# Local q and k loaded heads side by side and turned by transposes, half of the strided v on GpSimd's queue, one warming product per unit

## The chip, the cores and the metric

The kernel runs on one core of a Trainium2 chip. The metric is the device time of one execution in microseconds (us). Three runs of the kernel before took 1207.23 to 1209.63 us, with a median of 1208.55.

## The reference

An attention layer with two kinds of masked heads feeds two mixture-of-experts layers. Only the attention is touched by the change:

```python
scores = scale * np.matmul(q, k.transpose(0, 1, 3, 2))     # 4 x 8 heads x 576 x 576, head size 64
mask_local = (rel >= 0) & (rel < 32)
mask_strided = (rel >= 0) & (pos[None, :] % 32 == pos[:, None] % 32)
masks = np.stack([mask_local if h < H // 2 else mask_strided for h in range(H)], axis=0)
...
attn = attn / (np.sum(attn, axis=-1, keepdims=True) + 1e-09)
return np.matmul(attn, v)
```

Heads 0 to 3 are local (each query sees the 32 keys up to itself), heads 4 to 7 strided (each sees the keys at its own place modulo 32). The first mixture gives each token to one of 8 experts, with 288 places each, in the order of the logits; the second weighs 4 experts by given shares. All is in float32.

## The kernel before

The function `front` computes the attention of 4 batches in 40 units, 10 for each batch: 5 strided ones (two groups of 108 or 126 rows each), then 5 local ones. A loop over t runs them as a software pipeline. In step t PE does, in this order: warming products, the transposes of the probabilities of unit t-4 (`tr_p`, line 222), the products with v of unit t-5 (`av`, lines 235 and 242), rows and logits of finished units, one piece of q or k (`pre`), the scores of unit t (lines 186 and 189), and one more piece. GpSimd (POOL) scales the probabilities of unit t-2 (`norm`, line 215), ScalarE (ACT) takes the exponentials of unit t-1 (`exps`, line 205), VectorE (DVE) adds the mask and finds the maximum (line 196). [...]

A piece (`piece`) turns a part of q or k so that the head size stands in the partitions. There are 16 for a batch: 8 strided ones, four transposes each (line 153), and 8 local ones, six products with the identity each (line 164). A copy on DVE or ACT (`copy`, lines 134 to 140) then takes the result out of PSUM into its place. The pieces of batch 0's strided heads stand ahead of the loop, those of its local heads in steps 1 to 4. The other batches' pieces begin with the seventh step of the batch before: four steps with strided pieces, four with local ones.

The loads are issued by `load_qk` (q and k: `qs`, `ks` strided, `ql`, `kl` local), `load_v` (strided v, `vs`) and `load_vl` (local v, `vl`), all on SP's queue. Batch 0 and the q, k of batch 1 come first; from then on step 10b+2 issues q, k of batch b+2 and strided v of batch b+1, step 10b+6 the local v of batch b+1. The program gives each load of a queue one of eight semaphores in turn, and a load waits for the one eight before it on its queue.

Warming products (`keep_busy`, line 409) multiply a constant tile `hot` and are read by nobody; they go to the PSUM tile `xr`, of which there are two buffers, shared with rows, logits and tokens. Before, they stand in steps 0 to 7 and, after the 40 units, in steps 41 to 44.

After the front a search on DVE picks the tokens of the experts (lines 522 to 746), the rows go to DRAM, and `experts` does the rest in an order that a planner made when the program was built.

Of the kernel before, what the change touches and what calls it, by code (L numbers as in the profile page):

```python
# [18 lines left out]
FT = mybir.dt.float32  # L19
# [15 lines left out]
def dap(t, off, *dims):  # L35
    return bass.AP(tensor=t.tensor, offset=t.offset + off, ap=[list(d) for d in dims])

def front(tc, ident, hot, q, k, v, wg, dp, xd, L, ready, hold, deferred):
    nc = tc.nc
    B, H, S, D = q.shape  # L40
    hs = S * D
    with ExitStack() as st:
        cst = st.enter_context(tc.tile_pool(name="fc", bufs=1))
        ld = st.enter_context(tc.tile_pool(name="fl", bufs=2))
# [6 lines left out]
        def load_qk(b, kinds="sl"):  # L51
            T = LD.setdefault(b, {})
            if "s" in kinds:
                for nm in ("qs", "ks"):
                    T[nm] = ld.tile([72, 32, 64], FT, name=nm)
            n = 8 if b == 0 else 32
            for r in range(0, 32 if "s" in kinds else 0, n):
                for nm, src in (("qs", q), ("ks", k)):
                    nc.sync.dma_start(T[nm][:, r:r + n].rearrange("p r d -> p (r d)"), dap(src, (b * H + 4) * hs + r * D, [hs, 4], [32 * D, 18], [1, n * D]))
            for nm, src in (("ql", q), ("kl", k)) if "l" in kinds else ():  # L60
                T[nm] = ld.tile([96, 4, 6, 64], FT, name=nm)
                nc.sync.dma_start(T[nm].rearrange("p h r d -> p h (r d)"), dap(src, b * H * hs, [6 * D, 96], [hs, 4], [1, 6 * D]))

        def load_v(b, lo=0, hi=10):
            T = LD[b]
            if not lo:
                T["vs"] = ld.tile([126, 10, 128], FT, name="vs")
            for t, (b0, n) in list(enumerate(zip(starts, sizes)))[lo:hi]:
                p = 0
                while p < n:  # L70
                    h, rp = divmod(b0 + p, 16)
                    m = min(n - p, 16 - rp)
                    nc.sync.dma_start(T["vs"][18 * p:18 * (p + m), t], dap(v, (b * H + 4 + h) * hs + 2 * rp * D, [2 * D, m], [32 * D, 18], [1, 2 * D]))
                    p += m

        def load_vl(b):
            T = LD[b]
            T["vl"] = ld.tile([96, 9, 256], FT, name="vl")
            nc.gpsimd.memset(T["vl"][:32, 0], 0.0)
            nc.sync.dma_start(T["vl"][32:, 0].rearrange("p (h d) -> p h d", d=D), dap(v, b * H * hs, [D, 64], [hs, 4], [1, D]))  # L80
            for h in range(4):
                nc.sync.dma_start(T["vl"][:, 1:, 64 * h:64 * h + 64], dap(v, (b * H + h) * hs + 32 * D, [D, 96], [64 * D, 8], [1, D]))

        load_qk(0)
        load_v(0, 0, 6)
        load_qk(1, "s")
# [33 lines left out]
        units = []  # L120
# [7 lines left out]
        def copy(out, in_, scale=None, eng="p"):  # L128

            flip[0] += 1  # L130
            ch = side_of[eng]
            if ch == "a" or (ch == "f" and flip[0] % 2):
                if scale is None:
                    nc.scalar.copy(out, in_)
                else:
                    nc.scalar.activation(out, in_, AF.Copy, scale=scale)
            elif scale is None:
                nc.vector.tensor_copy(out, in_)
            else:
                nc.vector.tensor_scalar(out, in_, scale, None, op0=OP.mult)  # L140

        def piece(b, i):

            j, i = divmod(i, 8)
            p = ps.tile([128, 512], FT, name="tr", bufs=2)
            sc = 0.125 if j == 0 else None
            if i < 4:
                if i == 0:
                    (QS, KS)[j][b] = wk.tile([128, 4, 16, 18], FT, name=("qS", "kS")[j])
                src, dst = LD[b][("qs", "ks")[j]], (QS, KS)[j][b]  # L150
                for a in range(4):
                    r = 8 * i + 2 * a
                    nc.tensor.transpose(p[:, 72 * a:72 * a + 72], src[:, r:r + 2, :].rearrange("p r d -> p (r d)"), ident[:72, :72])  # L153
                copy(dst[:, :, 4 * i:4 * i + 4, :].rearrange("p h r j -> p r h j"), p[:, :288].rearrange("p (r h j) -> p r h j", r=4, h=4), sc, "q" if sc else "p")
            else:
                hp, a = divmod(i - 4, 2)
                if i == 4:
                    (QL, KL)[j][b] = wk.tile([128, 2, 576 + 32 * j], FT, name=("qL", "kL")[j])
                    if j:
                        nc.gpsimd.memset(KL[b][:, :, :32], 0.0)  # L160
                src, dst = LD[b][("ql", "kl")[j]], (QL, KL)[j][b]
                for t in range(3):
                    for x in range(2):
                        nc.tensor.matmul(p[64 * x:64 * x + 64, 96 * t:96 * t + 96], src[:, 2 * hp + x, 3 * a + t, :], ident[:96, :96], start=True, stop=True)  # L164
                copy(dst[:, hp, 32 * j:].rearrange("p (s a t) -> p a t s", a=2, t=3)[:, a], p[:, :288].rearrange("p (t s) -> p t s", t=3), sc, "q" if sc else "r")

        def shape(n):
            b, kind, g = units[n]
# [141 lines left out]
        def logits(n):  # L310
            b, kind, g = units[n]
            if kind or g not in (2, 4):
                return
            i0, m = (0, 128) if g == 2 else (128, 160)
            p = LP[n] = ps.tile([128, 512], FT, name="xr", bufs=2)
            for h in range(4):
                nc.tensor.matmul(p[32 * h:32 * h + 32, :m], wgs[:, h], XTS[b].rearrange("p h j r -> p h (j r)")[:, h, i0:i0 + m], start=True, stop=False)
            if n < N - 1:
                logits_local(n)
# [42 lines left out]
        N = len(units)  # L362
        ORDER = (0, 8, 1, 9, 2, 10, 3, 11, 4, 6, 12, 14, 5, 7, 13, 15)
        p = ps.tile([128, 512], FT, name="pt")
# [9 lines left out]
        for t in range(N + 14):  # L374
            t_now[0] = t
            if t < N and t % 10 == 2 and units[t][0] + 1 < B:
                if units[t][0] + 2 < B:
                    load_qk(units[t][0] + 2)
                load_v(units[t][0] + 1)
                nxt = [(units[t][0] + 1, i) for i in ORDER]  # L380

            if t < N and t % 10 == 6 and units[t][0] + 1 < B:
                load_vl(units[t][0] + 1)
            if t == 28:
                side = cst.tile([128, 18, 8], FT, name="side")
                nc.gpsimd.memset(side, 0.0)
                nc.gpsimd.iota(side.bitcast(I32)[:, :, 4], pattern=[[1, 18]], base=0, channel_multiplier=18)
                rs = cst.tile([128, 18], FT, name="rs")
                nc.vector.tensor_reduce(rs, pr, AX.X, OP.add)
                nc.vector.tensor_scalar(rs, rs, 1e-9, None, op0=OP.add)  # L390
                nc.vector.reciprocal(rs, rs)
                nc.vector.tensor_tensor(side[:, :, :4], pr, rs[:, :, None].to_broadcast([128, 18, 4]), OP.mult)
                nc.gpsimd.dma_start(dap(xd, 512, [18 * XW, 128], [XW, 18], [1, 8]), side)
            if t % 10 == 6:
                todo += nxt
                nxt = []

            def at(d, f):
                if 0 <= t - d < N:
                    f(t - d)  # L400

            def pre():
                if todo and t:
                    piece(*todo.pop(0))

            def keep_busy(n):
                p = ps.tile([128, 512], FT, name="xr", bufs=2)
                for i in range(n):
                    nc.tensor.matmul(p, hot[:, :128], hot, start=True, stop=True)

            if BUSY[0] <= t < BUSY[1]:
                keep_busy(BUSY[2] + 2 * (t < 2))
            at(4, tr_p)
            if N < t < N + 5:
                keep_busy(2)
            at(2, norm)
            while late2:
                x = late2.pop(0)
                if x is None:
                    break  # L420
                x()
            while late:
                late.pop(0)()
            if t == N + 4:
                logits(N - 1)
            at(5, av)
            rows("o")
            if t < N:
                at(10, logits)
            elif t == N + 3:  # L430
                logits(N - 3)
            elif t == N + 5:
                logits_local(N - 1)
            pre()
            at(1, exps)
            rows("s")
            if t < N:
                scores(t)
            pre()
# [941 lines left out]
```

## Time and profile before

| | |
|---|---|
| median of three runs | 1208.55 us |
| the profiled execution, its own time | 1208.96 us |
| its span, first to last instruction | 1207.2 us |
| PE busy | 1177.4 us (98%) |
| DVE busy | 853.9 us (71%) |
| ACT busy | 621.8 us (52%) |
| POOL busy | 422.9 us (35%) |
| loads of the hardware queue | 188664 packets, 141.74 MB |

The busy times are sums over the whole span. The front takes about the first tenth of it, the routing search the next 45 us, the experts the rest. A stage is read from its own window: which engine is full there, at which granted clock, and what ends the waits of the others. PE's rows in a timeline give the start of a group and a duration that contains the latency of overlapping products; the distance from one start to the next is what a group holds PE for. A product in float32 leaves two records, a transpose one.

### The profile page before, as it was taken

The page shows a single profiled execution, that of the slowest core. Times are in us where ns is not written, and L with a number is a line of the kernel's source. Part 1 is how long each engine was busy: PE and PEld are TensorE (multiplying, and loading weights), DVE is VectorE, ACT ScalarE, POOL GpSimd, SP SyncE. Part 2 cuts the span into 40 slices and gives each one's busy share as a digit, 9 for nine tenths or more (in the row PEclk, how much of TensorE's full clock was granted, in tenths as well). Part 3 has the DMA queues.
Part 4 walks back from the last instruction along what each step waited for, and adds up shares of the span by engine and source line. Part 5 has one row for each costly group of instructions (what it writes and reads, how often), then busy time and mean ns, then how long its engine had stood idle before and what let it go on. Part 6 is the DMA issues. An engine that isn't in the chain of part 4 may idle for free.

```text
span 1207.2 us, 24909 instructions
## 1 busy us (share of the span) xinstructions
PE 1177.4 (98%) x9088; PEld 1038.6 (86%) x9095; DVE 853.9 (71%) x2248; ACT 621.8 (52%) x1602; POOL 422.9 (35%) x453
## 2 busy tenths in 40 slices
PE   9999799999999999999999999999999999999997
PEld 6777588898888888899999988999888999899996
DVE  5777677777785877778765588767877766766673
ACT  5898455542441442455545455555555555555552
POOL 4343030100000101001012565565755556756553
PEclk9999899999999999999999999999999999999999
DMA  8761564553252452475665433333433333333320
GB/s 187 181 151 39 172 203 147 163 166 99 88 160 81 136 156 56 141 226 170 191 204 156 127 90 102 98 100 102 125 103 89 105 105 105 123 106 102 98 81 36
DMA packets 191955, 152.98 MB, mean 127 GB/s; under 512 B 27640, under 2 KB 158776, under 8 KB 191400
## 3 DMA queue, kind: packets, MB, share of 16 engines
q1 hardware_dynamic: 188664, 141.74, 40.2%
q0 software_dynamic: 3168, 9.65, 2.5%
q8 instruction: 71, 1.16, 0.4%
q14 instruction: 52, 0.43, 0.1%
HBM read 141.77 MB, written 9.58 MB: 125 GB/s over the span
## 4 chain that ended last, share of the span: by engine, by line
PE 82%; DVE 7%; issue 3%; ACT 3%; DMA 2%; POOL 2%; SPq 0%; POOLq 0%; DVEq 0%; ACTq 0%
PE o L971 35%; PE h L971 18%; PE h L1201 16%; DVE wl L746 3%; DMA raw<-in_moe_w_dram 2%; PE tr L164 2%; PE pt L222 1%; PE pa L601 1%; PE tr L153 1%; PE av L242 1%; PE s L186 1%; PE av L235 1%; ACT hh L864 1%; POOL wl L1190 1%; DVE u L746 1%
## 5 line engine op out<-in xcount | busy, mean ns | idle before, releaser
L746 DVE TENSOR_TENSOR wl<-raw,wh 128x512 fp32r<-128x512 f32 x352 | 272.0, 804 | 4.6 <-ACT wh L844 3.8
L971 PE MATMUL o<-wl,hh 128*128 128x512 f32 x576 | 227.8, 395 | 0.0
L971 PE MATMUL o<-wh,hh 128*128 128x512 f32 x576 | 227.7, 395 | 0.0
L971 PE MATMUL o<-wh,hl 128*128 128x512 f32 x576 | 226.5, 393 | 0.0
L864 ACT ACTIVATE hh<-h 128x256 fp32r<-128x256 f32 (+1 forms) x208 | 81.7, 393 | 241.2 <-PE h L971 221.4
L844 ACT CAST wh<-raw 128x512 fp32r<-128x512 f32 x272 | 160.0, 619 | 59.8 <-DMA raw<-in_moe_w_dram 57.7
L1190 POOL TENSOR_TENSOR wl<-raw,wh 128x512 fp32r<-128x512 f32 x96 | 122.5, 1298 | 194.8 <-ACT wh L1189 194.7
L746 DVE SCALAR_TENSOR_TENSOR hl<-h,hh 128x256 fp32r<-128x256 f32 (+1 forms) x208 | 89.8, 432 | 103.6 <-ACT hh L864 102.4
L891 POOL DMA_INDIRECT xg<-xd,idx x24 | 26.3, 1095 | 367.0 <-DVE idx L746 285.0
L971 PEld LDWEIGHTS o<-wh,hl 128*128 128x128 f32 x576 | 108.6, 188 | 23.3
L1201 PE MATMUL h<-hold,wh 128*128 128x256 f32 x640 | 120.9, 282 | 1.4 <-DVE u L746 1.1
L1201 PEld LDWEIGHTS h<-hold,wh 128*128 128x128 f32 x640 | 107.9, 188 | 15.8 <-DVE u L746 2.8
L746 DVE SCALAR_TENSOR_TENSOR hl<-u,hh 128x256 fp32r<-128x256 f32 x144 | 83.0, 576 | 46.5 <-ACT hh L864 46.5
L1176 ACT CAST wh<-sums 128x512 fp32r<-128x512 f32 x96 | 59.8, 622 | 106.9 <-POOL sums L1164 70.6
L971 PEld LDWEIGHTS o<-wl,hh 128*128 128x128 f32 x576 | 108.6, 189 | 6.0
L971 PEld LDWEIGHTS o<-wh,hh 128*128 128x128 f32 x576 | 108.5, 188 | 6.1
L864 ACT ACTIVATE hh<-u 128x256 fp32r<-128x256 f32 x144 | 59.9, 416 | 103.3 <-DVE u L746 103.2
L746 DVE TENSOR_TENSOR u<-h,u 128x256 f32<-128x256 f32 x144 | 60.2, 418 | 62.9 <-PE h L1201 55.5
L746 DVE TENSOR_TENSOR wl<-sums,wh 128x512 fp32r<-128x512 f32 x96 | 74.7, 779 | 36.7 <-ACT wh L1176 36.7
L1201 PE MATMUL h<-hold,wl 128*128 128x256 f32 x320 | 89.8, 281 | 0.0
L971 PE MATMUL h<-xh,wh 128*128 128x288 f32 x256 | 76.1, 297 | 0.0
L971 PE MATMUL o<-hh,wl 128*128 128x288 f32 x256 | 76.0, 297 | 0.0
(271 smaller groups left out, 2927.2 us busy)
## 6 DMA issues: line engine op xcount, KB each, us to landing
raw<-in_moe_w_dram SPq DMA_DIRECT2D x464, 256.0 KB
vl<-in_v_dram SPq DMA_DIRECT2D x16, 192.0 KB
ql<-in_q_dram SPq DMA_DIRECT2D x4, 576.0 KB
kl<-in_k_dram SPq DMA_DIRECT2D x4, 576.0 KB
qs<-in_q_dram SPq DMA_DIRECT2D x3, 576.0 KB
ks<-in_k_dram SPq DMA_DIRECT2D x3, 576.0 KB
xd<-y SPq DMA_DIRECT2D x2, 576.0 KB
xd<-hl SPq DMA_DIRECT2D x5, 192.0 KB
```

The lines of the kernel that those rows point to most:

```text
L153: nc.tensor.transpose(p[:, 72 * a:72 * a + 72], src[:, r:r + 2, :].rearrange("p r d -> p (r d)"), ident[:72, :72])
L164: nc.tensor.matmul(p[64 * x:64 * x + 64, 96 * t:96 * t + 96], src[:, 2 * hp + x, 3 * a + t, :], ident[:96, :96], start=True, stop=True)
L186: nc.tensor.matmul(out[:rows], lt, rt, start=True, stop=True)
L222: nc.tensor.transpose(p[:keys, rows * j:rows * j + rows], T["p"][:rows, j, :keys], ident[:rows, :rows])
L746: return f(*args, **kw)
L844: nc.scalar.copy(c["h"][:, sl], c["raw"][a])
L864: nc.scalar.activation(hi, src, AF.Relu)
L891: nc.gpsimd.indirect_dma_start(out=xg[:, k, :], out_offset=None, in_=xd, in_offset=bass.IndirectOffsetOnAxis(ap=idx[:, k:k + 1], axis=0))
L971: nc.tensor.matmul(out, a, b, start=start, stop=stop)
L1176: nc.scalar.copy(S["W"][nm][0], src[nm]())
L1190: nc.gpsimd.tensor_tensor(l, r, h.bitcast(FT), OP.subtract)
L1201: mmx = lambda o, a, b, first, lastm, n: (nc.tensor.matmul(o, a, b, start=first, stop=lastm, skip_group_check=True), tick(n / 2315 + 0.009))
```

## The change

Local q and k are loaded with the four heads side by side in each row, by four loads of 256-byte runs in place of one with runs of 1536 bytes. A local piece is now three transposes of two heads at once in place of six products of one head, and its copy writes runs of three neighbours. From batch 1 on, the strided v of groups 5 to 9 (six of thirteen loads) is issued by GpSimd. The strided v stands ahead of q and k in step 10b+2. Steps 8 to 39 get one warming product each, ahead of `tr_p`.

```diff
             for nm, src in (("ql", q), ("kl", k)) if "l" in kinds else ():
-                T[nm] = ld.tile([96, 4, 6, 64], FT, name=nm)
-                nc.sync.dma_start(T[nm].rearrange("p h r d -> p h (r d)"), dap(src, b * H * hs, [6 * D, 96], [hs, 4], [1, 6 * D]))
+                T[nm] = ld.tile([96, 6, 4, 64], FT, name=nm)
+                for h in range(4):
+                    nc.sync.dma_start(T[nm][:, :, h, :], dap(src, (b * H + h) * hs, [6 * D, 96], [D, 6], [1, D]))
...
-                    nc.sync.dma_start(T["vs"][18 * p:18 * (p + m), t], dap(v, (b * H + 4 + h) * hs + 2 * rp * D, [2 * D, m], [32 * D, 18], [1, 2 * D]))
+                    (nc.gpsimd if b and t > 4 else nc.sync).dma_start(T["vs"][18 * p:18 * (p + m), t], dap(v, (b * H + 4 + h) * hs + 2 * rp * D, [2 * D, m], [32 * D, 18], [1, 2 * D]))
...
                 for t in range(3):
-                    for x in range(2):
-                        nc.tensor.matmul(p[64 * x:64 * x + 64, 96 * t:96 * t + 96], src[:, 2 * hp + x, 3 * a + t, :], ident[:96, :96], start=True, stop=True)
-                copy(dst[:, hp, 32 * j:].rearrange("p (s a t) -> p a t s", a=2, t=3)[:, a], p[:, :288].rearrange("p (t s) -> p t s", t=3), sc, "q" if sc else "r")
+                    nc.tensor.transpose(p[:, 96 * t:96 * t + 96], src[:, 3 * a + t, 2 * hp:2 * hp + 2, :].rearrange("p h d -> p (h d)"), ident[:96, :96])
+                copy(dst[:, hp, 32 * j:].rearrange("p (s a t) -> p a s t", a=2, t=3)[:, a], p[:, :288].rearrange("p (t s) -> p s t", t=3), sc, "q" if sc else "r")
...
             if t < N and t % 10 == 2 and units[t][0] + 1 < B:
+                load_v(units[t][0] + 1)
                 if units[t][0] + 2 < B:
                     load_qk(units[t][0] + 2)
-                load_v(units[t][0] + 1)
                 nxt = [(units[t][0] + 1, i) for i in ORDER]
...
             if BUSY[0] <= t < BUSY[1]:
                 keep_busy(BUSY[2] + 2 * (t < 2))
+            elif t < N:
+                keep_busy(1)
             at(4, tr_p)
```

On PE, in step 11 (a strided unit with local pieces of k; `s` are scores, `pt` is `tr_p`, `av` the products with v, `tr` a piece), the order before was:

```order
L222 MATMUL pt<-ident,pr 96x128 x4
L242 MATMUL av<-pT,vl 64x64 x8
L287 MATMUL xr<-ident,hold 96x128 x4
L164 MATMUL tr<-ident,kl 64x96 x6
L186 MATMUL s<-kS,qS 126x126 x4
L164 MATMUL tr<-ident,kl 64x96 x6
L222 MATMUL pt<-ident,pr 96x128 x4
```

and is now:

```order
L409 LDWEIGHTS hot
L409 MATMUL xr<-hot 128x512
L222 MATMUL pt<-ident,pr 96x128 x4
L242 MATMUL av<-pT,vl 64x64 x8
L287 MATMUL xr<-ident,hold 96x128 x4
L164 MATMUL tr<-ident,kl 128x96 x3
L186 MATMUL s<-kS,qS 126x126 x4
L164 MATMUL tr<-ident,kl 128x96 x3
L409 LDWEIGHTS hot
L409 MATMUL xr<-hot 128x512
L222 MATMUL pt<-ident,pr 96x128 x4
```

The two pieces shrink from six products to three transposes each, and a warming product stands ahead of the transposes of the probabilities of each step.

On SP, between the strided v of batch 0 and its local v, the order before was:

```order
L59 DMA qs<-in_q_dram 72x2048
L59 DMA ks<-in_k_dram 72x2048
L73 DMA vs<-in_v_dram 108x1x128
L73 DMA vs<-in_v_dram 36x1x128
L73 DMA vs<-in_v_dram 72x1x128
L73 DMA vs<-in_v_dram 108x1x128 x2
L62 DMA ql<-in_q_dram 96x4x384
L62 DMA kl<-in_k_dram 96x4x384
L80 DMA vl<-in_v_dram 64x4x64
```

and is now:

```order
L59 DMA qs<-in_q_dram 72x2048
L59 DMA ks<-in_k_dram 72x2048
L74 DMA vs<-in_v_dram 108x1x128
L74 DMA vs<-in_v_dram 36x1x128
L74 DMA vs<-in_v_dram 72x1x128
L74 DMA vs<-in_v_dram 108x1x128 x2
L63 DMA ql<-in_q_dram 96x6x64 x4
L63 DMA kl<-in_k_dram 96x6x64 x4
L81 DMA vl<-in_v_dram 64x4x64
```

The first issue of the local v of batch 0 stands behind six more issues here, and behind six more at the start, where the local q, k of batch 0 are split in the same way.

On POOL, between the constants and the first norms, there were no loads of v:

```order
L116 DMA wgs<-in_moe_w_gate_dram 64x4x8 x2
L119 DMA dpr<-in_moe_domain_probs_dram 128x72
L215 TENSOR_TENSOR pr<-pr,r 126x4x126
L160 MEMSET kL 128x2x32
L215 TENSOR_TENSOR pr<-pr,r 126x4x126
```

and now the six of batch 1 stand there:

```order
L117 DMA wgs<-in_moe_w_gate_dram 64x4x8 x2
L120 DMA dpr<-in_moe_domain_probs_dram 128x72
L74 DMA vs<-in_v_dram 108x1x128 x2
L74 DMA vs<-in_v_dram 36x1x128
L74 DMA vs<-in_v_dram 72x1x128
L74 DMA vs<-in_v_dram 108x1x128 x2
L215 TENSOR_TENSOR pr<-pr,r 126x4x126
L161 MEMSET kL 128x2x32
```

Those of batches 2 and 3 stand in the same way ahead of the norm of steps 12 and 22. The order of the instructions after the front is the same on every engine.

## Rows read from the trace of the kernel before

**Rows 1.** Windows: stretch, us, busy PE, PEld, DVE, ACT, POOL, granted clock, DMA share, GB/s

```profile
12.00:36.00 24.00, 23.48 (x338) 17.25 (x340) 16.53 (x112) 18.97 (x85) 7.60 (x10) 1.00 0.83 186
36.00:103.00 67.00, 66.81 (x1098) 52.48 (x1096) 51.99 (x314) 58.78 (x258) 23.62 (x33) 1.00 0.66 151
103.00:116.00 13.00, 12.44 (x215) 9.24 (x216) 8.95 (x74) 12.91 (x63) 5.86 (x7) 1.00 0.01 2
116.00:165.00 49.00, 40.37 (x407) 29.68 (x406) 30.88 (x114) 23.95 (x60) 10.58 (x9) 0.90 0.58 172
```

**Rows 2.** Timeline of PE, steps 24 and 29 to 31: start us, us, group

```profile
75.89 0.65 PE L222 MATMUL pt<-ident,pr 126*126 126x126 f32 x4
...
88.74 0.47 PE L153 MATMUL tr<-ident,qs 72*128 72x72 f32 x4
89.14 0.40 PE L189 MATMUL s<-kL,qL 64*64 64x96 f32 x8
89.46 0.47 PE L153 MATMUL tr<-ident,ks 72*128 72x72 f32 x4
89.77 0.60 PE L222 MATMUL pt<-ident,pr 128*96 128x128 f32 x4
...
92.35 0.72 PE L164 MATMUL tr<-ident,ql 96*64 96x96 f32 x12
92.99 0.64 PE L222 MATMUL pt<-ident,pr 128*96 128x128 f32 x4
93.56 0.69 PE L242 MATMUL av<-pT,vl 96*64 96x64 f32 x16
94.08 0.67 PE L164 MATMUL tr<-ident,kl 96*64 96x96 f32 x12
94.68 0.71 PE L186 MATMUL s<-kS,qS 64*126 64x126 f32 x8
```

**Rows 3.** Timeline of PE around step 7, with the first strided k of batch 1

```profile
27.57 0.47 PE L153 MATMUL tr<-ident,ks 72*128 72x72 f32 x4
27.88 0.60 PE L409 MATMUL xr<-hot 128*128 128x512 bf16 x2
28.32 0.53 PE L222 MATMUL pt<-ident,pr 108*108 108x108 f32 x4
```

**Rows 4.** Timeline of ACT at the end of the front: [idle before, releaser]

```profile
102.27 0.58 ACT L134 COPY pT<-pt 126x504 f32<-126x504 f32 x1 [0.43 <-PE pt L222]
```

**Rows 5.** SP's queue: issues of the local v of batch 0, and a wait

```profile
25.01 0.69 SPq L80 DMA_DIRECT2D vl<-in_v_dram  x1
25.74 6.98 SPq L82 DMA_DIRECT2D vl<-in_v_dram  x4
...
SPq L80 <- DMA ks<-in_k_dram: 2.9, 1, 2.9
```

**Rows 6.** Windows of two stretches with loads, columns as in rows 1

```profile
53.10:57.50 4.40, 4.40 (x83) 3.29 (x79) 4.11 (x30) 3.97 (x19) 2.35 (x4) 1.00 1.12 221
66.20:72.20 6.00, 5.99 (x106) 4.73 (x104) 5.39 (x29) 4.56 (x20) 1.07 (x3) 1.00 0.75 163
```

**Rows 7.** Timeline of POOL: its issues of loads, and the first norm

```profile
7.70 0.96 POOL L110 DMA_DIRECT2D wgl<-in_moe_w_gate_dram  x1 [0.31 <-POOL wgl L109]
...
10.49 0.57 POOL L119 DMA_DIRECT2D dpr<-in_moe_domain_probs_dram  x1
17.02 1.03 POOL L215 TENSOR_TENSOR pr<-pr,r 126x504 f32<-126x504 f32 x1 [5.96 <-DVE r L214]
```

**Rows 8.** Timeline of POOL in steps 21 and 22

```profile
68.84 0.15 POOL L160 MEMSET kL<- 128x64 f32 x1
71.73 1.29 POOL L215 TENSOR_TENSOR pr<-pr,r 126x504 f32<-126x504 f32 x1 [2.74 <-ACT hold L134]
```

**Rows 9.** Groups of instructions, 12 to 165 us: busy us, mean ns of one

```profile
L138 DVE COPY kL<-tr 128x288 f32<-128x288 f32 x16 | 10.7, 671 | 1.4 <-PE tr L164 1.3
...
L134 ACT COPY kS<-tr 128x288 f32<-128x288 f32 x12 | 4.7, 389 | 0.0
```

## The prediction

> **What bounds the kernel now.** The change touches only the attention front, so the first question is where the front ends and who sets its pace. I read the table of windows first [rows 1]. From 36 to 103 us TensorE (PE) is busy 66.81 of 67.00 us at a granted clock of 1.00, the 2.4 GHz level. ScalarE (ACT) is nearly as full, 58.78 us; VectorE (DVE) has 51.99, GpSimd (POOL) 23.62. A busy PE is not yet a bound PE, so I went on to PE's timeline [rows 2]. There each group starts where the one before it has just been issued, and no row names a releaser: from 92.35 to 94.68 the starts follow at 0.64, 0.57, 0.52 and 0.60 us. A step of the unit loop therefore lasts as long as PE takes to issue it. **The front is paced by PE's issue**, and what counts is the distance between the starts, not the printed durations, which hold the latency of overlapping products.
>
> At the end this turns round. ACT's timeline has its last wait for PE just before 102.27 [rows 4]; in the next 13 us ACT is busy 12.91 us and PE only 12.44 [rows 1]. There the exponentials set the pace, and PE has room. After 116 us comes the routing search, PE 40.37 of 49.00 us, and then the experts. Neither changes in its order, and both hang on the logits at the end of the front, so I let a microsecond of the front be a microsecond of the kernel.
>
> **The change, part by part.**
>
> *The transposes.* A local piece now has six 64-column products; it will have three transposes of 96 columns. There are 32 pieces, two in each of 16 steps: one ahead of the scores, one after. The first takes 0.60 us from start to next start (94.08 to 94.68), the second 0.64 (92.35 to 92.99) [rows 2]. No row shows a 96-column transpose. The nearest are the strided pieces, four of 72 columns in 0.40 us ahead of the scores (88.74 to 89.14) and 0.31 after (89.46 to 89.77), and the four of 128 columns of tr_p in 0.57 (92.99 to 93.56) [rows 2]. One transpose is thus 0.10 or 0.08 us at 72 columns and 0.14 at 128. At 96, 43% of the way, I take 0.117 and 0.105, so three are 0.35 and 0.32. The step saves 0.25 + 0.32 = 0.57 us, and 16 steps 9.1 us. Bounds: at the price of 72 columns 0.71 a step, 11.4 in all; at that of 128 columns 0.43 a piece, so 0.38 a step, 6.1 in all.
>
> *The warming products.* Two cost 0.44 us on PE (27.88 to 28.32) [rows 3], one 0.22. They are added in 32 steps, ahead of tr_p. Where PE paces, each counts in full. The last five steps fall where ACT paces [rows 1, 4], and I give them nothing: what hides them is the exponentials still queued on ACT. 27 x 0.22 = 5.9 us. Bounds: all 32 paid, 7.0; six more hidden behind ACT, 4.6.
>
> The clock is at its upper level in every front window [rows 1], so the products can win nothing back there.
>
> *The loads.* A local load becomes four issues with runs of 256 bytes in place of one with runs of 1536. First the rate. From 53.1 to 57.5 us, where the local v comes in runs of 256 bytes, the queues moved 221 GB/s; from 66.2 to 72.2, by the order of SP's issues mostly local q, k in runs of 1536, 163 GB/s [rows 6]. The trace gives no reason to price the short runs higher. The Trainium skill's page "DMA: Bandwidth & Descriptors" (Specifications) asks for at least 512 bytes for line rate; by it these loads would slow, and the first row of that group disagrees.
>
> Next the issues. SP lets at most eight transfers stand open, since each waits for the one eight back; six more issues for batch 0 are now ahead of qs and ks of batch 1. At 0.69 us each, like the first local-v issue [rows 5], they are 4.1 us of SP, but for part of that time SP waits anyway. The trace shows where it bites: SP's local-v issue waits until 25.01 us for ks of batch 1 [rows 5], and PE first uses that ks at 27.57 [rows 3]. The slack is 2.56 us. The four faster steps ahead of it bring PE there 4 x 0.57 = 2.3 us sooner, and I let ks land 1.4 us later, a third of the extra issue time: PE stands for 2.3 + 1.4 - 2.56 = 1.1 us. Ends: nothing if ks is on time, 3.8 with the full 4.1 us. The local v of batch 0, issued until 32.72 us [rows 5], is next in line to be late, but PE will have lost half its lead by then.
>
> *The order.* v ahead of q, k concerns loads that are issued over 10 us before their use in batches 1 to 3; I cost it at nothing, and SP's issue time stays what it was, as 6 v issues leave each batch and 6 q, k issues come.
>
> *v on GpSimd's queue.* Six issues stand in POOL's program ahead of a norm, in the third step of batches 0 to 2. POOL's own issues took 0.96 and 0.57 us [rows 7]; I take 0.8, 4.8 us in all. In batch 0 they fall into the idle time from 11.06 to 17.02 [rows 7]. In step 22 POOL is free at 68.99, and the norm that would start at 71.73 has 1.29 us of work and is needed by tr_p at 75.89 [rows 2, 8]. It can start as late as 74.60, so 5.61 us are there: 0.94 us an issue. Hidden, with 1 us to spare; zero.
>
> *The copies.* A 288-element copy into stride 6 took 671 ns; one into runs of 18 took 389 [rows 9]. The new ones write runs of three but read PSUM 96 elements apart, which no row shows; I take 500, with 389 and twice 671 as the ends. They run on DVE and ACT, which both have idle time while PE paces [rows 1]; at the upper end ACT would get 7 x 0.7 = 4.7 us more over the front against 8.2 idle from 36 to 103. Zero on the path.
>
> **Sum.** -9.1 + 5.9 + 1.1 = -2.1 us. The profiled execution took 1208.96 us and would take 1206.9; it lies 0.4 above the median of the three runs, 1208.55, so the forecast for the median is **1206.5 us**. That is 0.17%, just inside the 0.2% (2.4 us) that a measurement of this kernel can tell from no change; its own range, from the unknown prices in it, is 1204 to 1209.
>
> **Rivals.**
>
> *The loads are on time and the transposes cheap.* For it: 221 GB/s on short runs. With 11.4 saved, 4.6 paid and no stall the change gives -6.8, so 1201.7; halfway there 1204. 0.18.
>
> *GpSimd's queue stops the norm (slower).* POOL works in order, so six issues hold the norm, the norm holds tr_p, tr_p holds PE. At 2 us an issue they take 12 us, 6.4 over the room of 5.61, in two batches 12.8: 1219.3. It gives slower from 1.31 us an issue on, where 2 x (6 x 1.31 - 5.61) eats both the 2.1 gained and the 2.4 of the bound. Against it: 0.57 and 0.96 [rows 7]. 0.08.
>
> *Local q, k come late (slower).* If 256-byte runs went at half the 163 GB/s, the 1.18 MB of a pair would take 14.4 us for 7.2, twice before the local v of batch 0; ks of batch 1 would stand 7.2 later, at 32.2, and PE, due at 25.3, wait 6.9 there, and about as long again at the local v: -9.1 + 5.9 + 13.8, near 1219. It gives slower from a stall of 5.6 us on (5.6 - 3.2 = 2.4), ks at 30.9. Against it the 221 GB/s. The Trainium skill's page "DMA: Bandwidth & Descriptors" would lead here. 0.08.
>
> *The products wait.* The warming products take turns in the two xr buffers with rows and logits, so a reader on ACT that is behind now holds PE at the head of a step. Ten waits of 0.3 us would give +3, near 1209.5. PE's rows show no such wait so far. 0.08.
>
> **How the numbers follow.** The forecast has 0.58, of it 0.20 beyond the bound (stall near zero, or transposes under 0.3 us) and 0.38 within. Faster: 0.20 + 0.18 = 0.38. Same: 0.38 + 0.05 of the waiting products = 0.43. Slower: 0.08 + 0.08 + 0.03 = 0.19. The range goes from the middle of the first rival less 1 us to partial stalls of the two slow ones: 1203.0 to 1212.0.
>
> **What would show it.** Right: local pieces on PE at 0.30 to 0.40 us from start to next start; one warming product 0.22 us ahead of each tr_p; a first idle stretch of PE of about 1 us ahead of the first ks pieces of batch 1, near 25 us; POOL's six issues under 1 us each and tr_p of step 24 unstopped; ACT without gaps over the last 13 us of the front; the same length of everything after it. Wrong: a granted clock under 1.00 between 36 and 103 us, PE waiting for POOL after the third step of a batch, PE waiting for the local q, k or v, copies so slow that ACT paces the whole front, or a local piece over 0.45 us.

## The result, and the profile after

The changed kernel takes **1215.96 us** (median of five runs, 1214.36 to 1218.17) against 1209.13 us for the kernel before in the same comparison. The ratio is 1.0055, 95% interval 1.0034 to 1.0076: slower by 0.55%, some 6.8 us, where 1206.5 us (1203.0 to 1212.0) was forecast. The profiled execution took 1214.36 us with a span of 1212.7, so 5.40 us more than the one before.

All of it lies in the front. The scores of the sixth, the twelfth and the last unit in the PE timeline of the kernel before:

```profile
24.70 0.56 PE L189 MATMUL s<-kL,qL 64*64 64x96 f32 x16
...
41.63 0.71 PE L186 MATMUL s<-kS,qS 64*126 64x126 f32 x8
...
112.77 0.40 PE L189 MATMUL s<-kL,qL 64*64 64x96 f32 x8
```

and of the twelfth and the last in that of the changed kernel, where the last start 5.43 us later (those of the sixth are the first line of the next timeline):

```profile
48.05 0.71 PE L186 MATMUL s<-kS,qS 64*126 64x126 f32 x8
...
118.20 0.40 PE L189 MATMUL s<-kL,qL 64*64 64x96 f32 x8
```

So "a microsecond of the front is a microsecond of the kernel" held for these two executions. The windows of the front, with the columns of [rows 1], show where the time went:

```profile
12.00:27.00 15.00, 12.34 (x140) 8.90 (x140) 11.02 (x78) 11.84 (x54) 7.87 (x12) 1.00 0.78 165
27.00:44.00 17.00, 16.14 (x130) 12.09 (x133) 5.29 (x36) 9.13 (x37) 3.31 (x4) 0.50 0.76 167
44.00:60.00 16.00, 15.94 (x200) 12.42 (x199) 12.31 (x74) 13.65 (x61) 8.44 (x13) 1.00 1.06 191
...
103.00:116.00 13.00, 12.78 (x200) 9.71 (x204) 9.98 (x76) 12.81 (x62) 5.81 (x6) 1.00 0.01 2
```

The granted clock is 0.50, the 1.2 GHz level, from 27 to 44 us. PE is busy 16.14 of those 17 us, so the busy column alone would show nothing wrong; the clock column does, and the 130 PE instructions against 200 in the 16 us that follow. Before, all of 12 to 103 us had 1.00 [rows 1]. What came ahead of the fall stands in the PE timeline, where a wait from about 0.15 us on is named in brackets:

```profile
22.13 0.56 PE L189 MATMUL s<-kL,qL 64*64 64x96 f32 x16
...
23.53 0.65 PE L235 MATMUL av<-pT,vs 126*64 126x126 f32 x8
24.37 0.47 PE L154 MATMUL tr<-ident,qs 72*128 72x72 f32 x4 [0.19 <-DMA qs<-in_q_dram]
24.77 0.56 PE L189 MATMUL s<-kL,qL 64*64 64x96 f32 x16
27.42 0.74 PE L154 MATMUL tr<-ident,ks 72*128 72x72 f32 x4 [2.09 <-DMA ks<-in_k_dram]
...
29.67 0.99 PE L235 MATMUL av<-pT,vs 108*64 108x108 f32 x8
...
31.26 0.92 PE L189 MATMUL s<-kL,qL 64*64 64x96 f32 x16
...
45.86 0.38 PE L409 MATMUL xr<-hot 128*128 128x512 bf16 x1
46.08 0.60 PE L222 MATMUL pt<-ident,pr 128*96 128x128 f32 x4
```

PE stands 2.09 us for ks of batch 1, and from there the same groups cost more: the product with v took 0.65 us at 23.53 and 0.99 at 29.67, the scores 0.56 and 0.92. The order of events in numbers, by the starts of the scores: in the sixth step they come 2.57 us earlier than before (22.13 against 24.70), in the twelfth 6.42 later (48.05 against 41.63), then 1 us is won back to the end (5.43). Of the 8.99 us lost between, 2.28 are the two waits and 0.88 four warming products, less some 0.7 for the first three local pieces, a step and a half (the saving of a step is measured below). About **6.5 us are the price of the low clock**, an estimate by what is left over.

Why ks came late is on SP's queue. Its timeline after:

```profile
4.16 3.97 SPq L63 DMA_DIRECT2D ql<-in_q_dram  x4
8.18 3.62 SPq L63 DMA_DIRECT2D kl<-in_k_dram  x4
11.84 6.32 SPq L74 DMA_DIRECT2D vs<-in_v_dram  x8
18.20 0.49 SPq L59 DMA_DIRECT2D qs<-in_q_dram  x1
18.74 0.36 SPq L59 DMA_DIRECT2D ks<-in_k_dram  x1
```

and before:

```profile
4.16 0.35 SPq L62 DMA_DIRECT2D ql<-in_q_dram  x1
4.56 0.48 SPq L62 DMA_DIRECT2D kl<-in_k_dram  x1
5.08 10.27 SPq L73 DMA_DIRECT2D vs<-in_v_dram  x8
15.40 0.48 SPq L59 DMA_DIRECT2D qs<-in_q_dram  x1
15.93 1.02 SPq L59 DMA_DIRECT2D ks<-in_k_dram  x1
```

The local loads of batch 0 now hold SP for 7.68 us in place of 0.92; 3.95 us of that come back from the waits inside the eight v issues (10.27 to 6.32). What is left, 2.8 us, is the delay of qs (15.40 to 18.20) and of ks. The other queue cost PE nothing, as forecast. POOL's six issues took 3.71 us; in batch 0 no norm had to wait for them, in the thirteenth step one did:

```profile
11.06 3.71 POOL L74 DMA_DIRECT2D vs<-in_v_dram  x6
16.22 1.03 POOL L215 TENSOR_TENSOR pr<-pr,r 126x504 f32<-126x504 f32 x1 [1.45 <-DVE r L214]
...
48.38 3.70 POOL L74 DMA_DIRECT2D vs<-in_v_dram  x6 [0.37 <-PE tr L164]
52.06 1.07 POOL L215 TENSOR_TENSOR pr<-pr,r 126x504 f32<-126x504 f32 x1
```

The norm at 52.06 starts as the issues end, 1.60 us after DVE was done with its `r` (50.46), and so does the one in step 22, at 79.28. The transposes that read them, `tr_p` at 54.67 and 81.06, show no wait.

### The profile page after: what moved, and what is told of

The parts are those of the page before. It is cut to its first block, busy times and chain, and to the rows that moved or that the text cites. A ratio compares the mean times of both kernels' runs of the same rounds, so it can differ in the third digit from the quotient of the medians.

```text
span 1212.7 us, 24427 instructions
## 1 busy us (share of the span) xinstructions
PE 1178.8 (97%) x8824; PEld 1038.5 (86%) x8839; DVE 852.0 (70%) x2248; ACT 622.3 (51%) x1602; POOL 433.4 (36%) x471
## 4 chain that ended last, share of the span: by engine, by line
PE 80%; DVE 6%; DMA 4%; issue 3%; ACT 3%; POOL 2%; SPq 1%; POOLq 0%; DVEq 0%; ACTq 0%
PE o L973 35%; PE h L973 18%; PE h L1203 16%; DVE wl L748 2%; DMA raw<-in_moe_w_dram 2%; PE pt L222 1%; PE pa L603 1%; DMA ks<-in_k_dram 1%; PE tr L154 1%; PE av L235 1%; PE av L242 1%; POOL wl L1192 1%; ACT hh L866 1%; PE s L189 1%; DVE u L748 1%
```

## The experiments

The theory after the result: SP's longer issue list makes ks of batch 1 late, the faster steps bring PE there sooner, PE stands, and the clock that falls behind the wait costs three times the wait. Rivals: the transposes that took the place of products let the clock fall by themselves (A); the wait and the copies cost the time, not the clock (C); GpSimd's loads take ks's transfer rate (D).

**e1: ks ahead.** In the changed kernel, q, k of batch 1 three tiles of v earlier.

```diff
-        load_v(0, 0, 6)
+        load_v(0, 0, 3)
         load_qk(1, "s")
-        load_v(0, 6)
+        load_v(0, 3)
```

> The changed kernel, with the strided q, k of batch 1 issued after the first three tiles of the strided v of batch 0 instead of after six (about 3 us of SP's issue time earlier). Theory (ks of batch 1 came 2.1 us late, PE stood, and the 1.2 GHz stretch that followed cost about 7 us): ks lands near 24 us, PE does not wait for it by more than 0.3 us near 25 us, the granted clock stays at 1.00 from 12 to 103 us, and the kernel takes 1205 to 1208, some 8 us less than the changed kernel. Rival A (the clock falls because transposes took the place of products, whatever PE waits for): the low stretch stays and the time stays near 1214 to 1216. Rival B (v of batch 0 is what binds): the wait moves to the strided v near 28 us with the same low clock, time 1212 or more.

Measured: 1217.38 us, ratio 1.0068 (1.0048 to 1.0089). A miss in time, but the place of the loss moved, much as rival B had it. The waits in the PE timeline of e1:

```profile
25.64 0.44 PE L235 MATMUL av<-pT,vs 126*64 126x126 f32 x4 [0.95 <-DMA vs<-in_v_dram]
...
35.84 0.45 PE L242 MATMUL av<-pT,vl 96*64 96x64 f32 x8 [0.50 <-DMA vl<-in_v_dram]
37.17 0.33 PE L242 MATMUL av<-pT,vl 96*64 96x64 f32 x2 [0.88 <-DMA vl<-in_v_dram]
38.11 0.45 PE L242 MATMUL av<-pT,vl 96*64 96x64 f32 x6 [0.61 <-DMA vl<-in_v_dram]
```

The wait for ks is gone; one for the strided v and three for the local v of batch 0 stand in its place, and the clock falls near 38 us instead, as this window shows:

```profile
38.00:42.00 4.00, 3.89 (x26) 3.19 (x26) 1.05 (x2) 1.73 (x7) 0.00 (x0) 0.57 0.52 105
```

In this execution (1212.47 us) that was short; in the other five the mean granted clock was 0.982 to 0.989 against 0.992 here, and the time up to 1220.08. Earlier ks alone mends nothing: the next load in SP's order is late.

**e2: more products.** The changed kernel with work on PE ahead of the wait.

```diff
-                keep_busy(BUSY[2] + 2 * (t < 2))
+                keep_busy(BUSY[2] + 2 * (t < 2) + 3 * (2 <= t < 6))
```

> The changed kernel with three more products (0.66 us) in each of the unit steps 2 to 5, 2.6 us of added work on PE just ahead of the wait for ks of batch 1; ks itself lands as late as before. Theory (the wait is what lets the clock fall, and the low clock is what costs): PE comes to ks when it is there or up to 0.3 us early, the granted clock stays at 1.00 through the front, and the kernel, with 12 products more, takes 1208 to 1210, about 7 us less than the changed kernel. Rival A (the clock falls because transposes take the place of products): some of the low stretch stays, 1212 to 1216. Rival C (the 2 us of waiting and the copies cost, not the clock): the time stays at 1215 to 1218.

Measured: 1210.35 us, ratio 1.0007 (0.9994 to 1.0019). Twelve added products make the kernel 5.6 us faster than the changed one. The same stretches of e2:

```profile
12.00:27.00 15.00, 14.63 (x152) 9.91 (x148) 10.42 (x69) 10.23 (x46) 7.49 (x12) 1.00 0.74 170
27.00:44.00 17.00, 16.42 (x226) 12.77 (x218) 10.92 (x72) 14.54 (x63) 6.54 (x11) 1.00 0.80 172
```

PE comes to ks at 27.16 us without a wait, the clock stays at 1.00, and 226 PE instructions fit where 130 did. ks is as late as ever (issued at 19.01 us), the transposes are all there. So it is the clock that costs: had the wait been the price, work in its place would have changed nothing. The fall goes with the wait here; that the added products hold the clock by themselves, e2 alone does not exclude, but e10 has no wait and no low clock without them.

**e3: all v on SP's queue.**

```diff
-(nc.gpsimd if b and t > 4 else nc.sync).dma_start(T["vs"]
+nc.sync.dma_start(T["vs"]
```

> The changed kernel with all strided v loads on SP's queue again. Theory (ks of batch 1 is late by the six more issues of the local q, k of batch 0 on SP): ks lands within 0.5 us of where it lands in the changed kernel, the wait and the low stretch stay, the time is within 3 us of the changed kernel. Rival D (GpSimd's v loads of batch 1, which run from 11 us on, take the transfer rate from ks): ks lands 1.5 us or more earlier, no low stretch, the time is 1206 to 1209.

Measured: 1213.10 us, ratio 1.0036 (1.0021 to 1.0051). In the profiled execution (1215.21 us) qs is issued at 17.79 us, PE waits 1.99 us for ks until 26.64, and the clock is at 0.59 from 24 to 36 us and 0.70 from 36 to 48. Rival D falls: without GpSimd's loads ks starts PE 0.78 us sooner, but PE is nearly as much sooner itself (its scores ahead of the wait start at 24.09 in place of 24.77).

**e10: batch 0 in the old way.** Only batches 1 to 3 have the new loads and transposes.

```diff
+                if b == 0:
+                    T[nm] = ld.tile([96, 4, 6, 64], FT, name=nm)
+                    nc.sync.dma_start(T[nm].rearrange("p h r d -> p h (r d)"), dap(src, b * H * hs, [6 * D, 96], [hs, 4], [1, 6 * D]))
+                    continue
```

> The changed kernel, but the local q, k of batch 0 are loaded in one issue each with runs of 1536 bytes and turned by products as before; batches 1 to 3 keep the new loads and transposes. Theory (the extra issues of batch 0 and PE's lead of its first steps make the wait): qs of batch 1 is issued near 15.4 us, ks lands near 25 us, PE does not wait, the clock stays at 1.00, and the kernel takes 1207 to 1210: against the kernel before, 8 steps less of the gain in batch 0 (-6.8 for 12 steps) and +5.9 for the products. Rival A (transposes in place of products let the clock fall): no low stretch near 27 us, but one in the steps of batch 1, 36 to 60 us, time 1212 to 1216.

Measured: 1210.75 us, ratio 1.0014 (1.0001 to 1.0027), 0.75 us above what was expected. qs is issued at 15.46 us, no load holds PE for over 0.3 us, and the clock is 1.00 from 24 to 103 us. So the six issues and the eight short pieces in batch 0 bring the loss; in batches 1 to 3 the same edits lower no clock, against rival A.

**f1: e10 without the warming products.**

```diff
-            elif t < N:
-                keep_busy(1)
```

> The kernel of e10 (batch 0 loaded and turned in the old way, batches 1 to 3 in the new) without the added warming products. Theory (PE paces the front, so each product costs its 0.22 us there, and the clock does not need them while PE is not made to wait): the front ends some 5 to 6 us earlier than that of e10, its clock stays at 1.00 from 36 to 103 us, and the kernel takes 1203 to 1206. Rival (the products hold the clock in steps that have transposes in place of products): without them a low stretch opens somewhere between 36 and 116 us and the time is 1209 or more. Third way: the time saved on PE is waited for at the loads again (local v of batch 0 near 37 us), half of the gain, 1206 to 1209.

Measured: 1206.93 us, ratio 0.9983 (0.9967 to 1.0000). The clock stays at 1.00 from 36 to 116 us without them. The last scores start at 107.55 us, 4.78 earlier than in e10 and 5.22 earlier than before: the products cost a little less than the 5.9 us that they were priced at, and the clock of the front does not need them. The time lies in the range of the third way: PE waits 0.80 us for the local v of batch 0 near 37 us (0.29 in e10), and of the 5.2 us of the front only 2.7 arrive in the median. A step with two local pieces, in the PE timeline of f1:

```profile
88.30 0.71 PE L194 MATMUL s<-kS,qS 64*126 64x126 f32 x8
88.94 0.47 PE L172 MATMUL tr<-ident,ql 96*128 96x96 f32 x3
89.24 0.60 PE L230 MATMUL pt<-ident,pr 128*96 128x128 f32 x4
89.77 0.69 PE L250 MATMUL av<-pT,vl 96*64 96x64 f32 x16
90.39 0.47 PE L172 MATMUL tr<-ident,kl 96*128 96x96 f32 x3
90.79 0.71 PE L194 MATMUL s<-kS,qS 64*126 64x126 f32 x8
```

The pieces take 0.30 and 0.40 us. From scores to scores it is 2.49; before it is 2.97, from this line to the last of [rows 2]:

```profile
91.71 0.71 PE L186 MATMUL s<-kS,qS 64*126 64x126 f32 x8
```

A step saves **0.48 us**: the product with v ahead of a piece takes 0.62 in place of the 0.52 of [rows 2] and gives 0.10 of the pieces' saving back.

**f2: only the products.** The kernel before with the two lines that f1 takes out.

> The kernel before with nothing but the added warming product in the 32 steps from the ninth on. Price taken in the prediction: 27 products of 0.22 us that count, five that lie behind the exponentials, +5.9 us (4.6 to 7.0): 1213 to 1216. Rival (later loads, or a higher clock in what follows, give part of it back): +1 to +4 us.

Measured: 1212.92 us, ratio 1.0021 (1.0012 to 1.0030), +3.3 us, under the 1213 to 1216 expected and within the rival's +1 to +4; what gives part back is not shown. Its last scores start at 117.31, 4.5 late, though it is 0.4 ahead until the eighth step: the products cost 4.9 us of the front, near the lower end of 4.6 to 7.0.

**f3 and g2: ks late in the kernel before.** Nothing is changed but the order of loads. f3:

```diff
-        load_v(0, 0, 6)
+        load_v(0)
         load_qk(1, "s")
-        load_v(0, 6)
```

> The kernel before with the strided q, k of batch 1 issued behind all strided v of batch 0 (five issues, about 3.8 us, later); no transpose, load shape or product is changed. Theory (a PE that waits for ks there loses the clock): ks lands 2.5 to 4 us later, PE waits 1 to 2 us for it near 27.5 us, a low stretch follows within a few us, and the kernel takes 1213 to 1219, several times the wait. Rival A (the low clock comes from the transposes of the changed kernel): the clock stays at 1.00, the time rises by the wait alone, to 1210 or 1211.

Measured: 1211.01 us, ratio 1.0021 (1.0001 to 1.0042, without the run of 1229.74). In the profiled execution (1210.73 us) PE waited and the clock did not fall:

```profile
28.82 0.47 PE L152 MATMUL tr<-ident,ks 72*128 72x72 f32 x4 [1.06 <-DMA ks<-in_k_dram]
```

From 29 to 46 us it is at 1.00, and the front ends later by about the wait, as rival A had it. Nine of the twelve runs took 1208.7 to 1212.9 us with a mean clock of 0.992 to 0.995; three took 1217.98, 1220.48 and 1229.74 with 0.986, 0.985 and 0.974. g2 puts two issues of the local v ahead as well:

```diff
+        load_v(0)
+        load_vl(0, 0, 1)
         load_qk(1, "s")
+        load_qk(1, "l")
+        load_vl(0, 1)
```

> The kernel of f3 (before, with nothing changed but the order of loads) with the strided q, k of batch 1 two issues later still, behind the first two of the local v of batch 0. In f3 PE waited 1.06 us and the profiled run kept its clock, though three of its twelve runs took 1218 to 1230 at a mean clock under 0.987. Theory (the longer the wait, the surer the fall of the clock, with transposes or without): PE waits 2 to 3.5 us for ks near 27.5 us, the clock falls to its lower level in most runs, mean clock 0.983 to 0.988, and the median is 1216 to 1222. Rival (it takes the changed kernel's transposes): the mean clock stays over 0.990 in most runs and the median is 1211 to 1213, the wait alone.

Measured: 1229.62 us, ratio 1.0149 (1.0114 to 1.0185), beyond what was expected. The PE timeline and the window behind the wait:

```profile
26.52 0.47 PE L154 MATMUL tr<-ident,qs 72*128 72x72 f32 x4 [0.49 <-DMA qs<-in_q_dram]
...
30.31 0.74 PE L154 MATMUL tr<-ident,ks 72*128 72x72 f32 x4 [2.83 <-DMA ks<-in_k_dram]
...
32.56 0.99 PE L236 MATMUL av<-pT,vs 108*64 108x108 f32 x8
```
```profile
29.00:46.00 17.00, 15.69 (x130) 11.59 (x130) 5.44 (x37) 9.52 (x39) 3.31 (x4) 0.51 1.00 203
```

It is the picture of the changed kernel, 130 PE instructions in 17 us at half the clock, in a kernel with none of the change's transposes, short runs and products. The front is 0.72 us ahead before and 9.49 behind after: 10.2 us for 3.3 us of waits, so 6.9 for the clock. So the clock falls behind a wait with nothing of the change in the kernel, against rival A. The profiled execution took 1220.86 us; most other runs of g2 had mean clocks of 0.974 to 0.977 and took 1229 to 1232 us; where their second stretch lies no profile shows.

**g3: issues or short runs?** The kernel before, its batch 0 local q, k in four issues of 1536-byte runs each.

```diff
+                if b == 0:
+                    for h in range(4):
+                        nc.sync.dma_start(T[nm][:, h].rearrange("p r d -> p (r d)"), dap(src, (b * H + h) * hs, [6 * D, 96], [1, 6 * D]))
+                    continue
```

> The kernel before with the local q, k of batch 0 loaded head by head, four issues each as in the change, but into the old layout, so that the runs stay 1536 bytes long. If the number of issues delays SP: qs of batch 1 is issued 1.5 us or more later than in before (15.40 us), toward the 18.20 us of the changed kernel. If it is the 576 short runs of an issue: each issue stays near 0.35 us and qs of batch 1 is issued within 0.7 us of 15.4 to 16.3 us, as in the two kernels with the old load. The time is within 2 us of before in either case, as PE is no earlier and has 2.5 us to spare at ks.

Measured: 1208.54 us, ratio 0.9995 (0.9982 to 1.0008). Neither answer alone: qs of batch 1 is issued at 16.78 us, half way from 15.40 to 18.20. By the tile kl, count, then min/median/max ns of one issue, first g3, then the changed kernel:

```profile
L64 SPq DMA_DIRECT2D kl<-in_k_dram x4: 312/312/312, 7.8 to 9.9; - x4
```
```profile
L63 SPq DMA_DIRECT2D kl<-in_k_dram x16: 630/639/4978, 8.2 to 76.4; - x16
```

Six more issues cost SP 1.4 us of the delay, and another 1.4 come with the new shape, an issue of which takes SP 0.63 us with 576 short runs where one of 96 long runs takes 0.31. The count of runs is not the rule: before, the same queue issued the 384 long runs of all four heads in 0.33 us at the least, and a strided v with at most 126 runs of 512 bytes takes 0.75 in the median. What sets an issue's time was not tried.

**f4, g1, h1: the waits taken away.** f4 is the changed kernel without the added products, with all v on SP, and

```diff
-nc.sync.dma_start(T[nm][:, :, h, :]
+(nc.scalar if nm == "kl" and b == 0 else nc.sync).dma_start(T[nm][:, :, h, :]
...
-        load_v(0, 0, 6)
+        load_v(0, 0, 5)
         load_qk(1, "s")
-        load_v(0, 6)
-        load_qk(1, "l")
+        load_v(0, 5)
         load_vl(0)
+        load_qk(1, "l")
```

> The changed kernel with its waits taken away: local k of batch 0 issued by ScalarE's queue (2.6 us of issues off SP), strided q, k of batch 1 one tile of v earlier, local v of batch 0 ahead of local q, k of batch 1, all strided v on SP's queue, and no added products. Theory: PE never waits for a load by more than 0.3 us, the clock stays at 1.00 through the front, the 9 us of the transposes are kept: 1199 to 1203. Rival (the transfer rate binds: what comes earlier pushes something else late): a wait of 1 us or more moves to the local q, k of batch 1 near 38 us, a low stretch follows, 1206 to 1213.

Measured: 1213.72 us, ratio 1.0032 (1.0006 to 1.0058). The rival held in kind, at the strided q, k of batch 2. The profiled execution is the slowest of the twelve (1221.13 us); five took 1206.81 to 1210.56 with mean clocks of 0.985 to 0.990. By the sixteenth step its front is 5.0 us ahead; then, in PE's timeline and the window behind it:

```profile
50.75 0.47 PE L154 MATMUL tr<-ident,qs 72*128 72x72 f32 x4 [0.80 <-DMA qs<-in_q_dram]
53.39 0.47 PE L154 MATMUL tr<-ident,ks 72*128 72x72 f32 x4 [1.68 <-DMA ks<-in_k_dram]
```
```profile
54.00:91.00 37.00, 37.00 (x326) 28.28 (x325) 17.36 (x108) 22.11 (x94) 7.44 (x10) 0.50 0.77 175
```

PE is busy 37.00 of 37 us and does so at half the clock. qs of batch 2 was issued at 44.02 us, behind 13 v issues that began at 33.87: the order that the change brought, and that was priced at nothing, here with all 13 on SP where the change has seven. g1 turns it back:

```diff
                 if units[t][0] + 2 < B:
-                    load_qk(units[t][0] + 2)
+                    load_qk(units[t][0] + 2, "s")
+                load_v(units[t][0] + 1)
+                if units[t][0] + 2 < B:
+                    load_qk(units[t][0] + 2, "l")
```

> The kernel of f4 with the order of the batch loads of before for the strided kinds: in the third step of a batch the strided q, k of the batch after next are issued ahead of the strided v of the next, the local ones behind. In f4 they stood behind 13 v issues on SP, PE waited 0.80 and 1.68 us for them near 51 and 53 us, and a low stretch of 37 us began. Theory: qs and ks of batch 2 are issued near 35 us, PE does not wait for them, no low stretch in the front, the front ends 7 to 8 us earlier than before, and the kernel takes 1200 to 1205. Rival (each wait taken away uncovers the next): PE waits over 1 us for another load, local v or local q, k of batch 1 or the strided v, with a low stretch behind it, 1207 to 1216.

Measured: 1207.92 us, ratio 0.9984 (0.9968 to 1.0001). The profiled execution (1213.06 us) is the second slowest; the fastest run took 1204.61 with a mean clock of 0.995. In the profiled one qs of batch 2 goes out at 34.36 us and no load holds PE until 84; there the local v of batch 2 does, for 1.74 us in three waits, and the clock is 0.52 from 85 to 110 us. h1 issues the local v ahead of the local q, k in batches 1 to 3 and gives GpSimd's queue its six v issues again:

```diff
-                if units[t][0] + 2 < B:
-                    load_qk(units[t][0] + 2, "l")
...
                 load_vl(units[t][0] + 1)
+                if units[t][0] + 2 < B:
+                    load_qk(units[t][0] + 2, "l")
```

> The kernel of g1 with two more moves: in batches 1 to 3 the local v is issued ahead of the local q, k of the batch after (both in the seventh step), and the last five tiles of the strided v go by GpSimd's queue again, as in the change, which takes six issues a batch off SP. In g1 SP issued the local v of batch 2 only at 81.04 us, behind 13 v and eight local q, k issues, PE waited 0.73, 0.36 and 0.65 us for it from 84 us on, and 23.9 us of the lower clock followed. Theory: the local v of batch 2 is issued near 75 us, no load makes PE wait over 0.4 us, the clock stays at 1.00 through the front, which ends some 8 us earlier than before; 2 us of that are lost again in the search, as in f1: 1201 to 1204. Rival (each wait taken away uncovers the next): a wait over 1 us and a low stretch at another load, 1206 or more.

Measured: **1202.41 us** (nine runs, 1200.52 to 1205.56), ratio 0.9937 (0.9917 to 0.9958): faster than both kernels. Its windows, against [rows 1], and its last scores:

```profile
12.00:36.00 24.00, 23.43 (x285) 17.46 (x288) 16.20 (x115) 20.25 (x91) 10.61 (x16) 1.00 0.80 174
36.00:103.00 67.00, 66.47 (x1002) 51.68 (x1001) 55.11 (x366) 63.87 (x292) 34.13 (x49) 1.00 0.74 157
```
```profile
104.57 0.40 PE L189 MATMUL s<-kL,qL 64*64 64x96 f32 x8
```

From 12.05 us, where PE waits 0.72 us for ks of batch 0, to the end of the front no load holds PE for as long as 0.15 us, and the front ends 8.20 us earlier than before. Its first scores start 1.50 us later than before (13.50 against 12.00), so from the first scores to the last it gains 9.70. Against the change, it keeps the transposes, their loads and GpSimd's half of v, drops the products, issues the local k of batch 0 on ScalarE's queue, and puts the loads in the order in which PE needs them.

## Why the prediction was wrong

**The step that failed** is the stall at ks of batch 1, "PE stands for 1.1 us", and with it the sentence that the clock is at its upper level in every front window, "so the products can win nothing back there". The mechanism was named rightly: extra issues on SP, PE sooner, ks just not there. Two sizes were off. PE waited 2.09 us (and 0.19 for qs), since SP's delay was 2.8 us and not a third of 4.1: ks let PE start at 27.42, 2.4 us and not 1.4 after the 25.01 of [rows 5]. And the wait was priced at its own length. The runs put 6.5 us of low clock behind it (6.9 in g2, where nothing differs but the order of loads), and in e2, where PE does not stand, none of it comes. A forecast of +1.1 with an upper end of 3.8 became 8.8. The front windows of before could not show this price, as no wait in its front was long; that their level need not hold once PE stands is what the sum left out. There was a sign in the last row of [rows 1], 0.90 behind the front, where PE does stand: in finer windows of before PE is busy 0.98 of the 4 us from 140 to 144, and the clock is 0.50 in the next 4 us.

The rest of the sum, term by term:

- *Transposes*, −9.1 us. The four steps ahead of the wait brought 2.29 us (11.72 to 22.13 after, 12.00 to 24.70 before), 0.57 each as taken, but with luck: a wait of 0.58 us for a copy is in it, and in e3, f4, g1 and h1 the same steps are 2.7 us shorter than before. With 0.48 a step in batches 1 to 3, where the product with v ahead of the piece is slower, it would be some 2.7 + 12 x 0.48 = 8.5 in all. h1, without the products and with its loads on time, takes 9.7 us less from its first scores to its last (91.07 for 100.77). The size was right, within the bounds of 6.1 to 11.4.
- *Warming products*, +5.9. One is 0.22 us on PE at the upper clock (45.86 to 46.08 after), and f2 has 4.9 us for all of them.
- *Copies*, hidden but for one: a kL copy is 453 ns in the median where 500 was taken, but in the third step a piece waited 0.58 us for one on DVE, until 16.53.
- *v on GpSimd's queue*, hidden: 0.62 us an issue, within 0.94. Two norms were held by 1.6 us, the `tr_p` behind them was not. That rival fell.
- *The order*, nothing: true in the changed kernel, where PE is late after 27 us. Where PE keeps its lead, with all v on SP, v ahead of q, k costs waits of 2.5 us and the clock behind them (f4, against g1); with six v issues on GpSimd's queue it was not tried.
- *ACT at the end*: 12.81 of 13 us from 103 to 116, as before.

Transposes and products alone would give −8.5 + 4.9, about −3.6 us, or −4.8 by the 9.7 of h1, where −3.2 was forecast. The rival "local q, k come late" had the right victim and the right sign, with the wrong cause (half the transfer rate) and the wrong point of decision: it asked for a stall of 5.6 us, and 2.1 did it. The Trainium skill's page "TensorE: Matmul & The Clock Gate" (section "HAM oscillation — how this bites in real kernels") describes this kind of loss, a PE that waits for a load and comes back at half the clock, and counts the penalty as half of the throttled time. By that, 17 us would cost an estimated 8.5. The trace agrees in kind and gives about 6.5. The Trainium skill's page "DMA: Bandwidth & Descriptors" (section "Issuing engines are not separate DMA queues") says that a second issuing engine saves only issue time, usually small relative to the transfer. Here issue time on SP was what decided: 2.8 us of delay for ks, with 0.63 us for an issue.

What stays open: f1, e10 and e2 end their fronts 5.2, 0.4 and 1.2 us earlier than before but gain 2.7 and lose 1.8 and 1.4 in the medians. The search behind the front has stretches at the lower clock before [rows 1] and after (0.90 from 116 to 165 us before, 0.86 in f1); whether an earlier front lengthens them was not tried. Nor does a trace show why the same program keeps its clock in one run and not in the next: by the mean clock f3 lost it in three of twelve, one run of e3 kept 0.993 (1208.39 us), and a run of the kernel before, beside h1, had 0.988 (1217.66 us).

## What to carry to other kernels

Price a wait of PE by what it does to the clock, not by its length: here 2.3 us of standing cost 8.8, and with 2.6 us of work put in its place the front ended 6.6 us earlier (e2). Before a stage is made faster, list the loads that it will now reach sooner, with the slack of each, and count what a load's issues take on the issuing queue: the delay hits whatever is issued behind it. After each wait that is taken away look for the next one; it took five moves in the loads until the gain of the transposes was kept.

## What the runs showed that was not expected

- A low stretch outlasts its wait many times over: 17 us after 2.1 and after 2.8 us of waiting, 37 us after waits of 0.80 and 1.68 (f4), with PE busy 92 to 100% of the time.
- With a wait of 1.06 us in the profiled run, nine of twelve runs kept their mean clock at 0.992 or more and three did not (f3).
- Issues on SP do not cost the same, and neither the bytes nor the count of runs alone gives the order: 0.31 us with 96 runs of 1536 bytes, 0.33 with 384 of them, 0.63 with 576 of 256 bytes, 0.75 with up to 126 of 512.
